# Taking P home earlier: both casts ahead of the exponential, the home transfer ahead of the outgoing one

## The chip, the cores and the metric

One core of one Trainium2 chip. The metric is the device time of one execution in microseconds (us); of the kernel before, three runs gave 974.37, 975.12 and 977.23 us, median 975.12 us. All tables and rows come from one profiled execution of it.

## The reference

Attention with a hashed mask, then a feed-forward block on its result, all in float32:

```python
q, k, v: (4, 8, 768, 64);  proj: (64, 6);  w_in: (512, 2048);  w_out: (2048, 512)
q_bits, k_bits = (q @ proj) > 0, (k @ proj) > 0        # six bits: a bucket of each row
mask   = q_bucket[..., :, None] == k_bucket[..., None, :]
scores = where(mask, q @ k.T / sqrt(64), -1e9)
attn   = exp(scores - max);  attn = attn / (sum(attn) + 1e-9)
x      = (attn @ v).transpose(0, 2, 1, 3).reshape(3072, 512)
h      = x @ w_in
out    = (h * clip(h + 3, 0, 6) / 6) @ w_out
```

## The kernel before

**Tiles and steps.** There are 32 heads (4 batches of 8) with 768 queries each, so 192 tiles of 128 queries, numbered g = 0 to 191; six make a head. The loop at line 1195 runs one step k for each tile, and each step works on several tiles at different stages: the scores of tile k+3 are multiplied on TensorE (PE; `scores`, lines 387 and 389), `lowest(k+2)` copies the scores of tile k+2 out of PSUM on VectorE (DVE) and takes each row's extreme (line 396, into a buffer `p` of which there are two), `exponential(k+2)` makes P of it on ScalarE (ACT, line 408). Products are kept near float32 by splitting each operand into a rounded high part and a low part that holds the rest, and adding the products.

**Turning P.** For the product with V, P has to lie with its keys on the partitions. Up to tile 101 the PE transposes it. From tile GT = 102 on (90 tiles) the DVE and two DMA trips do: `flip(g)` transposes P in blocks of 32 by 32 in place (line 429) and sends it to HBM, 384 KB, into one of four buffers `fd` (the outgoing transfer); `move(g)` brings it back, rearranged, with four transfers of 96 KB each (the home transfer, lines 442 to 448) into one of two SBUF buffers, named `spare` and `px` in the profile. Then `split_p(g, c)` splits each half: ACT casts the high part (line 475), and the low part is subtracted on GpSimd (POOL, line 477) for half c = 1 and on DVE (line 479, kept in `lows` until `split_lows` issues it) for c = 0. Two tiles together go to `values_whole` (line 505), twelve matmuls at line 513 at the beginning of an odd step, that use the high parts of half 1 first, then those of half 0, then the low parts.

**What runs beside.** In the same steps the feed-forward block of earlier rows runs, one of sixteen slices of the hidden width a step: `gemm1` (line 661), the gate (ACT at line 683, DVE at line 684), its split into `gb` (ACT at line 689, DVE at line 690), `gemm2` (lines 699, 700, 704). It is a generator in four stages: A is the split of the gate, B is `gemm1`, C is `gemm2` of the slice before together with the gate, D is side work for the next chunk of rows. After the attention ends, the rest of the feed-forward block runs alone.

**Order.** PE, DVE, ACT and POOL run in the order in which the code calls them (line 1099). All plain DMAs are issued by SyncE (SP, line 78) from one queue, in an order that a planner works out by its own estimates; `tc.issue_after(x)` obliges it to put what the block issues behind x in that queue. SP issues in order: when an instruction waits for its semaphores, all that is queued behind it waits too. Waits follow from the data: the home transfer of tile g waits for the landing of its `fd`, and for the low parts of tile g-2, which sat in the same SBUF buffer; `lowest(g)` waits until the outgoing transfer of tile g-2 has read its `p` buffer.

**One step before the change** (`beside_ffn`, line 1115, k > 102) calls, in this order: `values_whole` in odd steps; `lowest(k+2)` and then stage A (the other way round in steps with k % 6 == 2, `behind`); `exponential(k+2)`; side multiplies; `flip(k+2)` with its outgoing transfer; the cast and POOL's low part of half 1 of tile k-1; stage B; outputs; stage C, inside which (`amid`, between the gate's two instructions) the cast of half 0 and DVE's low part come; `lead(k+3)` with the scores; `move(k+1)`, tied behind the outgoing transfer of tile k+2; stage D.

Of the kernel before, what the change touches and what calls it, by code (L numbers as in the profile page):

```python
# [28 lines left out]
LA = 3  # L29
# [3 lines left out]
LT = 1  # L33
# [10 lines left out]
def lsh_attention_moe(  # L44
# [10 lines left out]
    nc = tc.nc  # L55
# [3 lines left out]
    KT = S // P  # L59
# [14 lines left out]
    last = None  # L74

    def dma(out: bass.AP, in_: bass.AP):
        nonlocal last
        last = nc.sync.dma_start(out=out, in_=in_)  # L78

    paced = False  # L80
# [147 lines left out]
    NS = NJ * KT  # L228
# [3 lines left out]
    GT = GF + FT  # L232
# [139 lines left out]
    scs, probs, outs = {}, {}, {}  # L372
# [18 lines left out]
    def lowest(g: int):  # L391

        s = scs.pop(g)
        m = sp.tile([P, 1], F32, name=f"m{g}", tag="m", bufs=4)
        pr_ = sp.tile([P, 2, HW], F32, name=f"p{g}", tag="p", bufs=2)
        nc.vector.tensor_scalar(  # L396
            out=pr_[:], in0=s[:, :, :HW], scalar1=CAP, scalar2=None,
            op0=ALU.min, op1=ALU.min, accum_out=m[:],
        )
        probs[g] = pr_, m  # L400
# [20 lines left out]

    written, moved, homes = {}, {}, []

    def flip(g: int):
        nonlocal written
        x = probs.pop(g)[0][:].rearrange("p c k -> p (c k)")
        nc.vector.transpose(x, x)  # L429
        d = dp.tile([P, S], F32, name=f"fd{g}", tag="fd", bufs=4)  # L430
        dma(out=d[:], in_=x)
        written[g] = d, last

    def move(g: int):
        if not homes:
            px = sp.tile([P, S], F32, name="px", tag="ga", bufs=1)
            homes.extend([spare[0][:, :S], px[:]])
        to = moved[g] = homes[g % 2]
        d, _ = written.pop(g)
        after = written[g + 1][1] if g + 1 in written else last  # L440
        with tc.issue_after(after.ins):
            for x in range(4):
                r = slice(32 * x, 32 * x + 32)
                dma(
                    out=to[r].rearrange("b (i c) -> b i c", i=4),
                    in_=d[:].rearrange("(i b) (g c) -> g b i c", i=4, g=4)[x],
                )

    lent = []

# [32 lines left out]
    def split_lows():  # L483
        for f in lows:
            f()
        lows.clear()
# [31 lines left out]
    adds, fresh = [], []  # L518
# [10 lines left out]
    def output(un: int):  # L529
        nonlocal vdone  # L530
        i, u = divmod(un, KT // 2)
        b, h = divmod(i, H)
        o = (h % 2) * D
        acc = accs.pop(un)

        if u != 1:
            outs[i] = sp.tile([P, 4 * P if u == 0 else 2 * P], F32, name=f"y{i}_{u}", tag=f"y{u}", bufs=1)
        y = outs[i][:, 2 * P :] if u == 1 else outs[i][:, : 2 * P]

        r = slice(o, o + D)  # L540
        r2 = slice(D - o, 2 * D - o)
        last_head = h == H - 1 and u == (0 if b else 2)
        if last_head:
            nc.scalar.copy(y[r], acc[r2])
            nc.vector.tensor_add(y[r], acc[r], y[r])
        else:
            nc.scalar.copy(y, acc[:])
        if u or last_head:
            single = last_head or h == H - 1 and b
            c = slice(2 * u * P, 2 * (u + 1) * P) if single else slice(0, 4 * P) if u == 1 else slice(4 * P, S)  # L550
            to = xs[b][h * D : (h + 1) * D, c]

            with tc.issue_after(copied.ins):
                dma(out=to, in_=y[r] if single else outs[i][r])
            if not last_head:
                ts = (u,) if single or u else (0, 1)
                (fresh if single and u == 2 else adds).append((i, ts if u != 1 or single else (0, 1), to, y[r2] if single else outs[i][r2]))
        vdone = 2 * un + 2


# [118 lines left out]
    def gate(n: str, fc: int, hg, copy, engine, between=lambda: None):  # L679

        hp, g = hg[:, 0], hg[:, 1]
        r = sp.tile([P, TC], F32, name=f"g{n}_{fc}", tag="g", bufs=1)
        nc.scalar.activation(r[:], hp, AF.Relu, bias=three[:], scale=1.0)  # L683
        nc.vector.scalar_tensor_tensor(out=g, in0=r[:], scalar=6.0, in1=hp, op0=ALU.min, op1=ALU.mult)  # L684
        between()

        def split():
            gh, gl = gate_tiles(f"{n}_{fc}")
            copy(gh, g)  # L689
            engine.tensor_sub(gl, g, gh.bitcast(F32))  # L690
            return gh, gl

        return split
# [31 lines left out]


    xr0, x0 = {}, {}
    side, opening, amid = [], [], []

    def beside():  # L730
        if side:
# [195 lines left out]
    def ffn():  # L927
# [5 lines left out]
        def there(c: int) -> bool:  # L933

            b, t = chunks[c]
            return vdone >= (b + 1) * HK - KT + 2 * (t + 1) and not pending(b, range(H), t)
# [40 lines left out]
        for c, (b, t) in enumerate(chunks):  # L977
            while not there(c):
                if pend is not None:
                    finish()()  # L980
                stage = "B"
                yield
            n = f"{b}_{t}"
            if c not in xr:
                begin(c)
            while side:
                beside()
                stage = "B"
                yield
                if not paced:  # L990
                    yield
            if c not in xhl:
                place(c)
                for cc in range(NCC):
                    split(c, cc)
            ffn_on = True
            copy = nc.scalar.copy
            po = None
            for fc in range(NFC):
                hp = gemm1(n, fc, xhl[c])  # L1000
                stage = "C"
                yield
                end = finish() if pend is not None else lambda: None
                if po is None:
                    po = ps.tile([P, 2, 512], F32, name=f"po{n}", tag="s" if b == B - 1 and t % 2 == 0 else "po", bufs=1)
                parted = paced
                split_g = gate(n, fc, hp, copy, nc.vector, lambda: amid and amid.pop()())
                if not parted:
                    gg = split_g()
                end()  # L1010
                if c + 1 < len(chunks) and c + 1 not in xr and there(c + 1):
                    if fc >= XF[chunks[c + 1][0] == B - 1]:
                        begin(c + 1)
                if parted:
                    stage = "D"
                    yield
                    for _ in range(-(-len(side) // (NFC - fc))):
                        beside()
                if fc + 1 == NFC and c + 1 in xr and c + 1 not in xhl and not side:
                    place(c + 1)  # L1020
                    for cc in range(NCC):
                        split(c + 1, cc)
                elif not parted:
                    beside()
                if parted:
                    stage = "A"
                    yield
                    gg = split_g()
                pend = ((b, t), (fc, [po[:, u] for u in range(2)], *gg))
                stage = "B"  # L1030
                yield
                if not parted:
                    beside()
            del xhl[c]
# [64 lines left out]
    with tc.manual_schedule(engines={ET.PE, ET.DVE, ET.Activation, ET.Pool}):  # L1099
# [15 lines left out]
        def beside_ffn(k: int):  # L1115
# [9 lines left out]
            for _ in range(2):  # L1125
                u = vnext // 2
# [6 lines left out]
                        through.append(vnext // 2 - 1)  # L1133
                if k < GT:
                    break
            behind = (k - 1 + LA) % KT == 4
            if GT <= k < NS - 2 and not behind:
                lowest(k + 2)
            go("A")
            if GT <= k < NS - 2 and behind:  # L1140
                lowest(k + 2)
            if k < GT:
                for c in range(2):
                    split_p(k, c, False)
                split_lows()
                while through:
                    output(through.pop(0))
                flip(k + 1)
# [9 lines left out]
            paced = True  # L1158
            multiply()
            if k + 2 < NS:  # L1160
                flip(k + 2)
            split = GT <= k - LT < NS
            if split:
                split_p(k - LT, 1, False)
            go("B")
            if k == NS + LT:
                homes.clear()
# [2 lines left out]
            hashed = k + LA < NS and (k + LA) % KT == 4 and (k + LA) // KT + 1 < NJ  # L1170
            if hashed:
                hash_qk((k + LA) // KT + 1)
            if split:
                amid.append(lambda: (split_p(k - LT, 0, False), split_lows()))
            go("C")
            while amid:
                amid.pop()()
            split_lows()
            if hashed:
                bits((k + LA) // KT + 1)  # L1180
            if k + LA < NS:
                lead(k + LA)
            if moves:
                moves.pop(0)()
            if GT <= k + 1 < NS:
                move(k + 1)

            place_in_chunk = (k - GT) % NFC
# [6 lines left out]
        for k in range(NS + LT + 2):  # L1195
# [4 lines left out]
            i, t = divmod(k, KT)  # L1200
# [74 lines left out]
        paced = False  # L1275
# [52 lines left out]
```

## Time and profile before

| | |
|---|---|
| three runs | 974.37, 975.12, 977.23 us |
| profiled execution | 973.11 us, span of its instructions 971.3 us |
| PE / weight loads / DVE / ACT / POOL busy | 948.0 / 873.6 / 723.5 / 625.0 / 473.6 us |
| stage with flips, 396.2 to 799.8 us | 90 flips, PE busy 396.77 of 403.60 us, DMA engines busy 0.82 |
| DMA traffic | 152.06 MB, mean 157 GB/s |

The PE row says how long matmuls were under way by a model of their ends, and the granted clock is 0.998 of the full one. The stage from 396.2 us to 799.8 us is the one that the change touches: 90 of the 192 steps. A row of the timeline gives the start and the length in us, then engine, line, operation, the tile written and the tile read, the shapes, how many instructions are merged into the row, and, in square brackets, how long the engine had been idle before and what ended that. DMA rows of SP are the issue of a transfer, not the transfer.

### The profile page before, as it was taken

The page shows a single profiled execution, that of the slowest core. Times are in us where ns is not written, and L with a number is a line of the kernel's source. Part 1 is how long each engine was busy: PE and PEld are TensorE (multiplying, and loading weights), DVE is VectorE, ACT ScalarE, POOL GpSimd, SP SyncE. Part 2 cuts the span into 40 slices and gives each one's busy share as a digit, 9 for nine tenths or more (in the row PEclk, how much of TensorE's full clock was granted, in tenths as well). Part 3 has the DMA queues.
Part 4 walks back from the last instruction along what each step waited for, and adds up shares of the span by engine and source line. Part 5 has one row for each costly group of instructions (what it writes and reads, how often), then busy time and mean ns, then how long its engine had stood idle before and what let it go on. Part 6 is the DMA issues. An engine that isn't in the chain of part 4 may idle for free.

```text
span 971.3 us, 19460 instructions
## 1 busy us (share of the span) xinstructions
PE 948.0 (98%) x6306; PEld 873.6 (90%) x6306; DVE 723.5 (74%) x1470; ACT 625.0 (64%) x1421; POOL 473.6 (49%) x582
## 2 busy tenths in 40 slices
PE   8999999999999999899999999999999999999997
PEld 7999888999989999799899899989899899889896
DVE  7999988888569999877878878878777874342422
ACT  6898875655478988667766666666666664333332
POOL 6777744665537776455555545555545432000000
PEclk9999999999999999999999999999999999999999
DMA  3567579100035554787898788788887772101000
GB/s 117 140 156 188 131 224 377 58 1 1 6 119 119 115 142 112 192 252 233 238 267 234 231 256 241 230 267 236 243 258 233 211 227 71 44 1 44 1 22 22
DMA packets 113613, 152.06 MB, mean 157 GB/s; under 512 B 13876, under 2 KB 82612, under 8 KB 113512
## 3 DMA queue, kind: packets, MB, share of 16 engines
q1 hardware_dynamic: 108472, 144.79, 48.8%
q0 software_dynamic: 5040, 6.03, 5.3%
q8 instruction: 50, 0.82, 0.4%
q14 instruction: 51, 0.42, 0.2%
HBM read 77.34 MB, written 54.00 MB: 135 GB/s over the span
## 4 chain that ended last, share of the span: by engine, by line
PE 79%; DVE 8%; DMA 4%; ACT 4%; issue 3%; POOL 1%; SPq 1%; ACTq 0%; DVEq 0%; POOLq 0%
PE h L661 25%; PE acc L500 6%; PE po L704 6%; PE po L699 6%; PE po L700 6%; PE acc L513 6%; PE pt L418 5%; PE s L389 5%; PE s L387 5%; DMA spare<-fd 2%; DVE p L396 2%; DVE pl L479 2%; ACT ph L475 1%; SPq L78 1%; DVE qq L352 1%
## 5 line engine op out<-in xcount | busy, mean ns | idle before, releaser
L408 ACT ACTIVATE p<-p,m 128x768 f32<-128x768 f32 x192 | 180.2, 939 | 113.4 <-DVE p L396 105.2
L396 DVE TENSOR_SCALAR_CACHE_REDUCE p<-s 128x768 f32<-128x768 f32 x192 | 182.7, 952 | 24.9 <-PE pt L418 12.4
L684 DVE SCALAR_TENSOR_TENSOR h<-g,h 128x256 f32<-128x256 f32 x192 | 81.1, 423 | 102.0 <-ACT g L683 99.0
L683 ACT ACTIVATE g<-h,three 128x256 f32<-128x256 f32 x192 | 91.2, 475 | 94.9 <-PE h L661 94.0
L661 PE MATMUL h<-xh,w 128*128 128x256 f32 x1024 | 146.8, 282 | 0.0
L661 PEld LDWEIGHTS h<-xh,w 128*128 128x128 f32 x1024 | 134.9, 188 | 4.2 <-ACT xh L650 0.6
L429 DVE STREAM_TRANSPOSE p<-p 128x768 f32<-128x768 f32 x90 | 88.1, 979 | 65.2 <-ACT p L408 65.1
L477 POOL TENSOR_TENSOR pl<-spare,ph 128x384 fp32r<-128x384 f32 x45 | 45.8, 1018 | 127.3 <-ACT ph L475 71.4
L479 DVE TENSOR_TENSOR pl<-pt,ph 128x384 fp32r<-128x384 f32 x196 | 100.0, 550 | 4.0 <-ACT ph L475 3.5
L387 PE MATMUL s<-kk,qq 76*128 76x384 f32 x384 | 100.5, 343 | 2.0 <-ACT kk L357 1.5
L389 PE MATMUL s<-kk,qq 128*128 128x384 f32 x384 | 100.4, 343 | 0.0
L700 PE MATMUL po<-w,gb 128*128 128x512 f32 x250 | 98.4, 393 | 0.0
L699 PE MATMUL po<-w,gb 128*128 128x512 f32 x250 | 98.3, 393 | 0.0
L475 ACT CAST ph<-pt 128x384 fp32r<-128x384 f32 x196 | 86.1, 474 | 14.3 <-PE pt L418 13.0
L216 POOL TENSOR_TENSOR w<-wr,w 128x128 fp32r<-128x128 f32 x128 | 71.9, 593 | 45.2 <-ACT w L210 41.9
L418 PE MATMUL pt<-ident,p 128*128 128x128 f32 x612 | 86.2, 275 | 1.9 <-DVE pl L479 1.1
L689 ACT CAST gb<-h 128x256 fp32r<-128x256 f32 x141 | 52.4, 372 | 54.5 <-DVE h L684 26.8
L661 PE MATMUL h<-xl,w 128*128 128x256 f32 x512 | 81.2, 280 | 0.0
L418 PEld LDWEIGHTS pt<-ident,p 128*128 128x128 f32 x612 | 72.5, 141 | 8.9 <-PE pt L418 1.5
L704 PE MATMUL po<-w,gb 128*128 128x512 f32 x250 | 78.6, 395 | 1.5 <-DVE gb L690 1.5
L318 POOL TENSOR_TENSOR kk<-raw,qq 64x192 fp32r<-64x192 f32 (+1 forms) x73 | 65.4, 920 | 25.1 <-ACT qq L304 21.7
L387 PEld LDWEIGHTS s<-kk,qq 76*128 76x128 f32 x384 | 66.6, 190 | 11.7 <-ACT kk L357 2.0
(153 smaller groups left out, 2150.9 us busy)
## 6 DMA issues: line engine op xcount, KB each, us to landing
fd<-p SPq DMA_DIRECT2D x90, 384.0 KB
spare<-fd SPq DMA_DIRECT2D x180, 96.0 KB
px<-fd SPq DMA_DIRECT2D x180, 96.0 KB
kk<-qq SPq DMA_DIRECT2D x62, 192.0 KB
wr<-in_w_in SPq DMA_DIRECT2D x16, 512.0 KB
wr<-in_w_out SPq DMA_DIRECT2D x16, 512.0 KB
raw<-in_qkT SPq DMA_DIRECT2D x19, 384.0 KB
vr<-in_v SPq DMA_DIRECT2D x32, 192.0 KB
```

The lines of the kernel that those rows point to most:

```text
L387: nc.tensor.matmul(s[:, c, :HW], lhsT=q1[:KM, us], rhs=half(k1[:KM], c), start=True, stop=False)
L389: nc.tensor.matmul(s[:, c, :HW], lhsT=q2[:, us], rhs=half(k2, c), start=False, stop=True)
L396: nc.vector.tensor_scalar(out=pr_[:], in0=s[:, :, :HW], scalar1=CAP, scalar2=None, op0=ALU.min, op1=ALU.min, accum_out=m[:],)
L408: nc.scalar.activation(pr_[:], pr_[:], AF.Exp, bias=m[:], scale=-1.0, accum_out=sms[b][:, t, h : h + 1])
L418: nc.tensor.transpose(pt[:, x], probs[g][0][:, c, x * P : (x + 1) * P], ident[:])
L475: nc.scalar.copy(hi, pt)
L479: lows.append(lambda: engine.tensor_sub(lo, pt, hi.bitcast(F32)))
L661: nc.tensor.matmul(hp, lhsT=wi[:, wp, wc], rhs=x[cc][xp], start=(k == 0 and cc == 0), stop=(k == 2 and cc == NCC - 1),)
L683: nc.scalar.activation(r[:], hp, AF.Relu, bias=three[:], scale=1.0)
L699: nc.tensor.matmul(po[u], lhsT=gh[:, us], rhs=wo[:, 0], start=(fc == 0), stop=False)
L700: nc.tensor.matmul(po[u], lhsT=gh[:, us], rhs=wo[:, 1], start=False, stop=False)
L704: nc.tensor.matmul(po[u], lhsT=gl[:, us], rhs=wo[:, 0], start=False, stop=(fc == NFC - 1))
```

## The change

Inside the steps k > 103, `halves_of(k-1)` now stands ahead of `exponential(k+2)`: both casts, POOL's low part of half 1 and DVE's of half 0. Right behind it `move(k+1)` issues the home transfer, so that it stands ahead of `flip(k+2)`, and `brought` ties the outgoing transfer of tile k+2 behind the last of the four home transfers. Before, the home transfer was tied behind that outgoing transfer. In step 103 the casts stay at the end of the step, and stage A comes ahead of `lowest(105)`. `amid` and its place in the gate go. The adding DMA of the last third of a batch's last head isn't held back by a turn any more in the stage beside the feed-forward block.

```diff
-    written, moved, homes = {}, {}, []
+    written, moved, homes, brought = {}, {}, [], []
     def flip(g: int):
...
-        dma(out=d[:], in_=x)
+        if brought:
+            with tc.issue_after(brought.pop().ins):
+                dma(out=d[:], in_=x)
+        else:
+            dma(out=d[:], in_=x)
         written[g] = d, last
     def move(g: int):
...
+        brought[:] = [last]
...
-                (fresh if single and u == 2 else adds).append(
+                (fresh if single and u == 2 and not paced else adds).append(
...
-                split_g = gate(n, fc, hp, copy, nc.vector, lambda: amid and amid.pop()())
+                split_g = gate(n, fc, hp, copy, nc.vector)
...
-            behind = (k - 1 + LA) % KT == 4
+            behind = (k - 1 + LA) % KT == 4 or k == GT + 1
             if GT <= k < NS - 2 and not behind:
                 lowest(k + 2)
             go("A")
             if GT <= k < NS - 2 and behind:
                 lowest(k + 2)
+            def halves_of(g: int):
+                for c in (1, 0):
+                    split_p(g, c, False)
+                split_lows()
+            split = GT <= k - LT < NS
+            if split and k - LT > GT:
+                halves_of(k - LT)
+                if k + 1 < NS:
+                    move(k + 1)
...
             if k + 2 < NS:
                 flip(k + 2)
-            split = GT <= k - LT < NS
-            if split:
-                split_p(k - LT, 1, False)
             go("B")
...
-            if split:
-                amid.append(lambda: (split_p(k - LT, 0, False), split_lows()))
             go("C")
-            while amid:
-                amid.pop()()
-            split_lows()
             if hashed:
                 bits((k + LA) // KT + 1)
+            if split and k - LT == GT:
+                halves_of(GT)
             if k + LA < NS:
                 lead(k + LA)
             if moves:
                 moves.pop(0)()
-            if GT <= k + 1 < NS:
+            if GT <= k + 1 < NS and not (split and k - LT > GT):
                 move(k + 1)
```

More of the change, by code (lines that the diff above doesn't have):

```diff
@@ L556, in output @@
                 ts = (u,) if single or u else (0, 1)
-                (fresh if single and u == 2 else adds).append((i, ts if u != 1 or single else (0, 1), to, y[r2] if single else outs[i][r2]))
+                (fresh if single and u == 2 and not paced else adds).append((i, ts if u != 1 or single else (0, 1), to, y[r2] if single else outs[i][r2]))
         vdone = 2 * un + 2
@@ L727, in lsh_attention_moe @@
     xr0, x0 = {}, {}
-    side, opening, amid = [], [], []
+    side, opening = [], []
     def beside():
```

## The prediction

> **What bounds the kernel now.** I read first the windows of busy time for the stage that the change touches, with the row of the flips, then what PE waited for in that stage.
>
> ```profile
> 396.20:799.80 403.60, 396.77 (x2573) 365.58 (x2572) 319.54 (x611) 268.02 (x628) 208.26 (x269) 1.00 0.82 241
> ```
>
> ```profile
> L429 DVE STREAM_TRANSPOSE p<-p x90: 968/978/982, 396.2 to 799.8; 128x768 f32<-128x768 f32 x90
> ```
>
> ```profile
> PE acc L513 <- ACT ph L475: 4.5, 9, 1.5
> PE po L704 <- DVE gb L690: 1.5, 2, 0.8
> PE z L334 <- ACT y L547: 0.2, 1, 0.2
> ```
>
> The first row is a stretch, its length, then the busy time of PE, weight loads, DVE, ACT and POOL, the clock, and the share of the DMA engines and GB/s. PE is busy for 396.77 of 403.60 us at the full clock, so it sets the pace; a step takes (799.8 - 396.2) / 89 = 4.535 us on average. All that PE waits for in this stage is 4.5 + 1.5 + 0.2 = 6.2 us, most of it the value matmuls waiting for ACT's casts, in nine of the 45 pairs. No rearrangement of ACT, DVE or SP can win more than about these 6 to 7 us. What it can lose is open, since the DMA engines are busy at 0.82 beside PE's 0.98.
>
> The timeline of one whole step (and the edges of its neighbours) shows the order:
>
> ```profile
> 604.09 0.51 ACT L475 CAST ph<-px 128x384 fp32r<-128x384 f32 x1
> ...
> 604.44 0.54 SPq L78 DMA_DIRECT2D fd<-p  x1
> ...
> 604.63 0.56 DVE L479 TENSOR_TENSOR pl<-px,ph 128x384 fp32r<-128x384 f32 x1
> ...
> 604.66 0.96 PE L513 MATMUL acc<-ph,vv 128*128 128x256 f32 x6
> ...
> 605.11 0.95 DVE L396 TENSOR_SCALAR_CACHE_REDUCE p<-s 128x768 f32<-128x768 f32 x1
> 605.24 0.36 ACT L689 CAST gb<-h 128x256 fp32r<-128x256 f32 x1
> 605.25 1.80 SPq L78 DMA_DIRECT2D px<-fd  x4
> ...
> 605.98 0.42 DVE L690 TENSOR_TENSOR gb<-h,gb 128x256 fp32r<-128x256 f32 x1
> ...
> 606.10 0.94 ACT L408 ACTIVATE p<-p,m 128x768 f32<-128x768 f32 x1 [0.50 <-DVE p L396]
> ...
> 607.03 0.50 ACT L475 CAST ph<-spare 128x384 fp32r<-128x384 f32 x1
> ...
> 607.16 0.98 DVE L429 STREAM_TRANSPOSE p<-p 128x768 f32<-128x768 f32 x1 [0.43 <-ACT p L408]
> ...
> 607.61 1.01 POOL L477 TENSOR_TENSOR pl<-spare,ph 128x384 fp32r<-128x384 f32 x1 [2.16 <-DMA px<-fd]
> ...
> 607.83 0.47 ACT L683 ACTIVATE g<-h,three 128x256 f32<-128x256 f32 x1 [0.30 <-PE h L661]
> ...
> 608.17 0.34 SPq L78 DMA_DIRECT2D fd<-p  x1
> 608.20 0.50 ACT L475 CAST ph<-spare 128x384 fp32r<-128x384 f32 x1
> ...
> 608.34 0.43 DVE L684 SCALAR_TENSOR_TENSOR h<-g,h 128x256 f32<-128x256 f32 x1 [0.20 <-ACT g L683]
> ...
> 608.74 0.56 DVE L479 TENSOR_TENSOR pl<-spare,ph 128x384 fp32r<-128x384 f32 x1
> ...
> 609.34 0.37 ACT L689 CAST gb<-h 128x256 fp32r<-128x256 f32 x1
> ...
> 609.87 0.96 DVE L396 TENSOR_SCALAR_CACHE_REDUCE p<-s 128x768 f32<-128x768 f32 x1 [0.57 <-PE s L389]
> ...
> 610.75 0.42 DVE L690 TENSOR_TENSOR gb<-h,gb 128x256 fp32r<-128x256 f32 x1
> ...
> 612.22 0.62 PE L704 MATMUL po<-w,gb 128*128 128x512 f32 x2
> ```
>
> Three things are to be seen. The cast of half 0 ends at 604.60 us and the value matmuls begin at 604.66: there is no slack, hence the nine waits. The home transfer is issued at 605.25 us, 0.06 us after the low part of its buffer ends (604.63 + 0.56 = 605.19). And the outgoing transfer of the step (604.44) stands before it on SP, so the two big transfers of a step overlap and neither waits for the other.
>
> **Part one: the casts and low parts move up.** No instruction is added: 2 x 0.50 us of ACT, 1.01 of POOL and 0.56 of DVE a step stand elsewhere. In the step above, ACT ends the gate's split at 605.60 and was idle for 0.50 us before the exponential; with the two casts there the exponential begins at about 606.6, 0.5 us late. DVE puts its low part behind line 690 and ends it at about 607.2 and the side multiply at 607.6; the flip begins at 607.7 for 607.16, also 0.5 late. The gate's first half waits for PE until 607.83 and ACT is free by 607.75, so it isn't late; its second half goes from 608.34 to 608.66, and the next split of the gate on ACT came at 609.34, so this 0.3 us is covered. If that cover were gone, it would cost 0.3 us in each of some 75 ordinary steps, 22 us. The casts now lie a half step and more ahead of the value matmuls, so the 4.5 us of PE's waits for them go. Part one is worth -4.5 us.
>
> **Part two: stage A ahead of `lowest(105)`, and the adding DMA.** At 405.08 us below, PE waits 0.80 us for a low part of the gate that stood behind a `lowest`; the swap in step 103 takes that wait away: -0.8 us. The adding DMA of one head goes out at the end of step 147 instead of 151, on POOL, which is busy for 208.26 of 403.60 us: nothing. The tail after 800 us is untouched.
>
> **Part three: the home transfer ahead of the outgoing one.** Four issues of SP are moved past one, and with them a wait. Before, SP issued "outgoing of tile k+2, home of tile k+1". After, it is "home of k+1, outgoing of k+2", and the home transfer of k+1 reads the `fd` that was sent out one step earlier, so SP stops until it has landed. That closes a ring with one step a turn: outgoing issue, its landing (L), four home issues, next outgoing issue. A step can't be shorter than L + reaction + four issues. Before, a whole home transfer and another outgoing one lay between, so the ring wasn't closed.
>
> The four issues, and a last store for a lower bound, from the rows of line 78:
>
> ```profile
> L78 SPq DMA_DIRECT2D spare<-fd x180: 302/442/887, 400.8 to 803.1; - x180
> L78 SPq DMA_DIRECT2D px<-fd x180: 302/448/2137, 404.0 to 805.9; - x180
> ...
> L78 SPq DMA_DIRECT2D out<-ob x18: 341/378/807, 269.1 to 968.2; - x18
> ```
>
> The median is 0.442 to 0.448 us, so four take 1.78 us (the row at 605.25: 1.80). The reaction is 0.06 us (604.63 + 0.56 to 605.25).
>
> L isn't a row of its own. It is read where something waited for it:
>
> ```profile
> 400.37 0.32 SPq L78 DMA_DIRECT2D fd<-p  x1
> 400.78 1.93 SPq L78 DMA_DIRECT2D spare<-fd  x4
> ...
> 403.72 0.96 DVE L396 TENSOR_SCALAR_CACHE_REDUCE p<-s 128x768 f32<-128x768 f32 x1 [0.45 <-DMA fd<-p]
> ...
> 405.08 0.73 PE L704 MATMUL po<-w,gb 128*128 128x512 f32 x2 [0.80 <-DVE gb L690]
> ```
>
> ```profile
> 456.37 0.53 SPq L78 DMA_DIRECT2D fd<-p  x1
> 457.00 3.26 SPq L78 DMA_DIRECT2D px<-fd  x4
> 460.36 0.38 SPq L78 DMA_DIRECT2D fd<-p  x1
> 461.68 1.25 SPq L78 DMA_DIRECT2D spare<-fd  x3
> ```
>
> ```profile
> SPq L78 <- DMA fd<-p: 0.8, 1, 0.8
> ```
>
> ```profile
> GB/s 0 0 0 0 0 0 0 0 0 0 0 0 0 0 0 0 216 402 448 371 402 140 77 309 448 433 371 325 16 0 0 0 0 0 0 0 0 0 0 0
> ```
>
> At 403.72 the DVE is released by a landing 403.72 - 400.37 = 3.35 us after its issue, with a home transfer pressing on right behind it. The third fence is what SP waited for between 460 and 463 us: the home transfer at 461.68 had waited 0.8 us for the `fd` issued at 456.37, so that L was 5.3 us, with four slow home issues and a second outgoing transfer in between. The last row is the traffic from 966 us to the end at 971.3 in 40 slices: the last store of 256 KB, issued at 968.2, has its last bytes in slice 29, at 966 + 29 x 0.1325 = 969.8, so even alone a smaller transfer took 1.6 us and its receipt.
>
> So L lies between 1.6 and 5.3 us, and the ring between 1.6 + 0.06 + 4 x 0.302 = 2.9 us (it never binds) and 5.3 + 0.06 + 1.78 = 7.1 us (+223 us). I take L = 3.0, near the 3.35: in the new order no home transfer presses on behind, but the four just issued run ahead of it. The ring is then 3.0 + 0.06 + 1.78 = 4.84 us, above the 4.535 of a step. Of the 87 home transfers in the new order (tiles 105 to 191) each step is longer by 0.305 us: 26.5 us. The first steps are absorbed: an outgoing transfer at 604.44 has until 609.87, when `lowest` takes its buffer, which is 5.43 - 3.0 = 2.4 us to spare, and the gate's low part (ends 611.17) is needed at 612.22, another 1.0; about 3 us in all. Behind that the casts wait for the home transfer, the exponential and the gate's first half stand behind the casts on ACT, and `gemm2` on PE waits for the gate; PE's 4.5 + 0.8 us of old waits then lie inside the longer step and can't be counted again. SP's other transfers (loads of q, k, v, x, the row copies) stand behind the waiting one too, and where the planner puts one between the four, its issue joins the ring.
>
> The Trainium skill, "DMA: Bandwidth & Descriptors", section "Rules for kernel authors", advises to issue a DMA early and wait on its semaphore late; the change does the opposite to the outgoing transfer. The same page of the Trainium skill, section "Anatomy of one DMA — SWDGE (gpsimd) path", has a fit of 2.0 us plus the bytes at 436 GB/s for DMAs that GpSimd issues; as an estimate, 384 KB would take 2.9 us, the ring 4.74 us and the sum 973.11 + 87 x 0.2 - 3 = 987.5 us. The row's 3.35 us lies above that fit.
>
> **Sum.** 973.11 + 26.5 - 3 = 996.6 us against the profiled execution's 973.11 us; the median of the runs is 2.0 us above that execution, so 999 us.
>
> **Rivals.**
>
> The ring doesn't bind (faster). With the DMA engines less crowded at the moment of the outgoing transfer, L would be 2.6 us or less and the ring 4.44 us, under the 4.535. From L = 2.7 (4.535 - 1.84) on downward only parts one and two are left: 973.11 - 4.5 - 0.8 = 967.8, with the runs' 2.0 about 970 us, and down to 966 with the other waits. For it: the last store's 1.6 us, and the steps with hashing, which are longer and let the ring catch up. Against: the 3.35 us in the row that is nearest, and the 3.26 us that four home issues took at 457.00.
>
> The two cancel (no change). At L = 2.8 the ring is 4.64 us: 87 x 0.105 = 9, less 3 absorbed, is 6 us later if the old waits are inside, and about even if part of them is still won: 973 to 979.
>
> The moved casts cost by themselves (slower, without the ring). If ACT's exponential being 0.5 us late reaches the gate after all, the 0.3 us of part one come due in 75 steps, less the 5.3 won: 973.11 + 22 - 5 + 2 = 992 us. Against it: 0.5 us between the gate's end and the next split on ACT.
>
> **How the numbers follow.** The ring that binds: 0.60. The ring that doesn't: 0.24. The cancelling: 0.08. The casts by themselves: 0.08. A change of under 0.3%, 2.9 us, can't be told from none here. That gives faster 0.24, same 0.08, slower 0.68. For the ring that binds, L = 2.85 gives 4.69 us and +10 (985 us), L = 3.4 gives 5.24 us and +58 (1033 us): 985 to 1033. The range for all, 967 to 1033, takes in the side on which the ring doesn't bind, and leaves out L above 3.4.
>
> **What would show it.** Right: SP's wait for `fd` grows from a few us to some 100 us or more; the spacing of the flips goes from 4.535 to about 4.8 us; ACT's casts wait for DMA of `spare` or `px`; PE waits at lines 699 or 704 for the gate; the DMA share falls. The wait of line 513 for the casts is gone in any case; if it is still there, part one is wrong. If the flips keep 4.5 us and SP has time left behind its wait for `fd`, the ring doesn't bind and L was taken too long. If the flips are slower while SP waits for low parts or flips instead of `fd`, the casts are to blame.

## The result and the profile after

The changed kernel takes 1027.64 us (six runs, 1022.45 to 1029.62) against 975.26 us of the kernel before (six runs, 974.37 to 977.23): a ratio of 1.0525, 95% interval 1.0496 to 1.0554. Its profiled execution took 1022.45 us with a span of 1020.7 us. It is 49.3 us longer than the profiled execution before, and the stage with the flips holds nearly all of that. First the windows of busy time for that stage of the changed kernel (stretch, length, then PE, weight loads, DVE, ACT, POOL, clock, DMA share, GB/s), and its flips:

```profile
397.00:848.00 451.00, 411.92 (x2576) 366.68 (x2575) 321.23 (x612) 273.75 (x629) 208.02 (x271) 0.98 0.73 215
```

```profile
L429 DVE STREAM_TRANSPOSE p<-p x90: 964/978/981, 397.1 to 848.2; 128x768 f32<-128x768 f32 x90
```

The flips are (848.2 - 397.1) / 89 = 5.069 us apart for 4.535 before, and 89 x 0.534 = 47.5 us is the difference of the stage. ACT, DVE and POOL are busy for about as long as before, PE for 15 us longer; the DMA engines' share fell from 0.82 to 0.73. The granted clock is 0.98 in this stage for 1.00 before, but that can't be the main cost: in the run with the gate first, below, it is 1.00 in the stage, and the loss is 47 us for 52. Now what SP, DVE, ACT and PE waited for in the stage of the changed kernel (us in total, times, longest). Lines behind 430 have moved by five at most: 475, 479, 690 and 704 are now 480, 484, 695 and 709.

```profile
SPq L78 <- DMA fd<-p: 112.1, 71, 4.4
```

```profile
DVE p L396 <- DMA fd<-p: 95.2, 59, 3.6
```

```profile
ACT ph L480 <- DMA px<-fd: 13.0, 14, 2.1
ACT ph L480 <- DMA spare<-fd: 12.4, 13, 1.9
```

```profile
PE po L709 <- DVE gb L695: 25.3, 27, 3.1
PE z L334 <- DVE gb L695: 6.1, 8, 2.5
...
PE acc L518 <- POOL pl L482: 0.7, 1, 0.7
```

The first two of these rows in the kernel before:

```profile
SPq L78 <- DMA fd<-p: 3.2, 6, 0.8
```

```profile
DVE p L396 <- DMA fd<-p: 0.5, 1, 0.5
```

SP's wait for outgoing transfers went from 3.2 us in six waits to 112.1 us in 71. The value matmuls (now line 518) no longer wait for ACT's casts. PE waits instead for the gate's low part (line 695), which stands on DVE behind a `lowest` that waits for the outgoing transfer. One turn of the ring in the timeline of the changed kernel:

```profile
516.75 0.38 SPq L78 DMA_DIRECT2D fd<-p  x1
516.99 0.98 DVE L429 STREAM_TRANSPOSE p<-p 128x768 f32<-128x768 f32 x1 [0.29 <-ACT p L408]
...
517.69 0.60 SPq L78 DMA_DIRECT2D kk<-qq  x1
...
519.64 1.73 SPq L78 DMA_DIRECT2D px<-fd  x4
519.65 0.96 DVE L396 TENSOR_SCALAR_CACHE_REDUCE p<-s 128x768 f32<-128x768 f32 x1 [1.36 <-DMA fd<-p]
...
521.47 0.38 SPq L78 DMA_DIRECT2D fd<-p  x1
```

The outgoing transfer issued at 516.75 lands at 519.51, by its semaphore events. SP has had nothing else to issue since 518.29 and waits for this landing: the home transfer that reads the buffer goes out at 519.64, 0.13 us behind it, and `lowest` begins on DVE at 519.65, behind the same landing. The flip of 516.99 ended at 517.97, but its own outgoing transfer stands behind the home transfer and goes out at 521.47, 3.5 us later. From one outgoing issue to the next it is 4.72 us here and 5.17 us on average, and at no point of this turn did SP wait for a flip.

### The profile page after: what moved, and what is told of

The parts are those of the page before. It is cut to its first block, busy times and chain, and to the rows that moved or that the text cites. A ratio compares the mean times of both kernels' runs of the same rounds, so it can differ in the third digit from the quotient of the medians.

```text
span 1020.7 us, 19507 instructions
## 1 busy us (share of the span) xinstructions
PE 963.4 (94%) x6306; PEld 873.9 (86%) x6306; DVE 726.9 (71%) x1470; ACT 630.2 (62%) x1421; POOL 471.4 (46%) x582
## 4 chain that ended last, share of the span: by engine, by line
PE 54%; DMA 18%; DVE 13%; issue 6%; SPq 5%; POOL 2%; ACT 2%; DVEq 0%; ACTq 0%; POOLq 0%
PE h L666 16%; DMA fd<-p 16%; PE acc L505 6%; PE pt L418 5%; SPq L78 5%; PE po L709 4%; DVE pl L484 4%; PE po L704 4%; PE po L705 4%; PE s L389 3%; PE s L387 3%; DVE p L396 3%; PE acc L518 2%; DMA px<-fd 1%; DVE gb L695 1%
## 5 line engine op out<-in xcount | busy, mean ns | idle before, releaser
L396 DVE TENSOR_SCALAR_CACHE_REDUCE p<-s 128x768 f32<-128x768 f32 x192 | 183.2, 954 | 116.9 <-DMA fd<-p 95.2
L709 PE MATMUL po<-w,gb 128*128 128x512 f32 x250 | 82.4, 411 | 25.3 <-DVE gb L695 25.3
L704 PE MATMUL po<-w,gb 128*128 128x512 f32 x250 | 99.0, 396 | 1.4 <-ACT gb L694 1.3
L705 PE MATMUL po<-w,gb 128*128 128x512 f32 x250 | 98.4, 394 | 0.0
L709 PEld LDWEIGHTS po<-w,gb 128*128 128x128 f32 x250 | 44.4, 188 | 47.6 <-DVE gb L695 39.4
```

The lines of the kernel that those rows point to most:

```text
L396: nc.vector.tensor_scalar(out=pr_[:], in0=s[:, :, :HW], scalar1=CAP, scalar2=None, op0=ALU.min, op1=ALU.min, accum_out=m[:],)
L704: nc.tensor.matmul(po[u], lhsT=gh[:, us], rhs=wo[:, 0], start=(fc == 0), stop=False)
L705: nc.tensor.matmul(po[u], lhsT=gh[:, us], rhs=wo[:, 1], start=False, stop=False)
L709: nc.tensor.matmul(po[u], lhsT=gl[:, us], rhs=wo[:, 0], start=False, stop=(fc == NFC - 1))
```

## The experiments

The ring theory was set against two rivals: that the moved casts cost by themselves, and that only DVE's order behind the two buffers of P costs. Times are medians, beside runs of the kernel before on the same chip.

**The ring opened, the casts kept early.** The home transfer stands behind the flip and its outgoing transfer again:

```diff
                 halves_of(k - LT)
-                if k + 1 < NS:
-                    move(k + 1)
...
                 flip(k + 2)
+            if split and k - LT > GT and k + 1 < NS:
+                move(k + 1)
```

(and `brought` is gone. In the kernel before, `move` was called at the end of the step.)

> Both casts stay ahead of the exponential as in the changed kernel, but the outgoing transfer of the step goes first again and the home transfer is tied behind it, right behind the flip. The theory is a ring on SP: an outgoing transfer, its landing, four home issues, the next outgoing transfer, closed once a step (5.07 us between flips in the changed kernel, 4.54 before). With the ring open it expects 967 to 972 us and flips 4.46 to 4.50 us apart, with the PE's waits at line 513 gone. The rival, that the moved casts delay ACT and DVE by themselves, expects the time to stay near the changed kernel's, 1010 to 1030 us.

Measured: 976.01 us against 974.6 us, ratio 1.0012, interval 1.0000 to 1.0024. The loss of 52 us is gone, so it belongs to the order on SP. But the gain that was expected of the casts isn't there either: the flips are 4.59 us apart and not 4.46 to 4.50. The waits of PE and ACT in this run, and DVE's low part:

```profile
PE po L704 <- DVE gb L690: 2.7, 3, 1.3
PE po L699 <- ACT gb L689: 1.9, 5, 0.6
PE acc L513 <- POOL pl L477: 1.1, 2, 0.7
```

```profile
ACT ph L475 <- DMA px<-fd: 43.5, 35, 2.2
...
ACT ph L475 <- DMA spare<-fd: 9.5, 13, 1.3
```

```profile
L479 DVE TENSOR_TENSOR pl<-spare,ph x45: 1059/1066/1210, 408.5 to 810.9; 128x384 fp32r<-128x384 f32 x45
L479 DVE TENSOR_TENSOR pl<-px,ph x45: 546/1067/1408, 410.9 to 813.7; 128x384 fp32r<-128x384 f32 x45
```

PE's 4.5 us of waiting for casts at line 513 are gone, but its waiting for the gate has grown from 1.5 us to 2.7 + 1.9 us. Standing ahead of the exponential, the casts wait 43.5 + 9.5 us for home transfers, and ACT's exponential and gate wait behind them. And DVE's low part takes 1.07 us (median) where it took 0.56 to 0.64 in the kernel before:

```profile
L479 DVE TENSOR_TENSOR pl<-spare,ph x45: 557/642/869, 407.0 to 808.1; 128x384 fp32r<-128x384 f32 x45
L479 DVE TENSOR_TENSOR pl<-px,ph x45: 557/559/1467, 412.7 to 810.9; 128x384 fp32r<-128x384 f32 x45
```

**Only the order on SP.** The kernel before with the outgoing transfer put behind the home transfer (`last` is the last of its four) from tile 106 on; the casts stay where they were:

```diff
+        if g > GT + 3:
+            waiting.append((g, d, x))
+            return
         dma(out=d[:], in_=x)
...
+    def send():
+        g, d, x = waiting.pop()
+        with tc.issue_after(last.ins):
+            dma(out=d[:], in_=x)
...
                 move(k + 1)
+            if waiting:
+                send()
```

> The kernel before with its casts where they were, and only the order on SP changed: from tile 106 on each outgoing transfer is tied behind the home transfer of the tile ahead of it, at the end of the step. The ring theory expects the changed kernel's pace without its casts, flips 5.0 to 5.3 us apart, 1015 to 1040 us. The rival of the casts expects 975 us.

Measured: 1042.68 us, ratio 1.0694 (1.0676 to 1.0712); its flips:

```profile
L429 DVE STREAM_TRANSPOSE p<-p x90: 968/978/982, 397.7 to 869.1; 128x768 f32<-128x768 f32 x90
```

```profile
SPq L78 <- DMA fd<-p: 93.9, 63, 4.1
```

That is (869.1 - 397.7) / 89 = 5.30 us a step. The order on SP alone makes the whole loss, without any cast moved. It is 15 us more than in the changed kernel. By the semaphore events the landing is 0.10 us longer there, the time from the landing to the first home issue 0.12 and the four issues 0.07; what makes them longer is open (SP's waits for DVE's low parts come to 2.8 us in all).

**Half of the home transfer behind the outgoing one.** `move` is called for two of its four transfers ahead of the exponential and for the other two behind `flip`:

```diff
-                    move(k + 1)
+                    move(k + 1, range(2))
...
                 flip(k + 2)
+            if split and k - LT > GT and k + 1 < NS:
+                move(k + 1, range(2, 4))
```

(and `brought` is emptied behind the second call.)

> The changed kernel with the home transfer cut in two on SP: two of its four transfers ahead of the outgoing one, two behind it. The ring has two issues of 0.44 us less: 5.17 less 0.9 is 4.3 us, under the 4.54 of a step, so the ring theory expects 968 to 982 us. The rival of the casts expects 1010 to 1030 us. A third theory, that only the two buffers of P matter, which come free when the outgoing transfer has left, expects a part of the loss back, 990 to 1010 us.

Measured: 993.35 us, ratio 1.0189 (1.0174 to 1.0204), with 4.81 us between flips. Two thirds of the loss come back, but not all: the time lies outside of the ring theory's range and inside of the third theory's. From one outgoing issue to the next it is 4.87 us instead of the expected 4.3. By the semaphore events the landing, which had been taken as unchanged, is 3.35 us on average here and 3.08 in the changed kernel, with two home transfers now right behind the outgoing one; the first home issue follows 0.41 us behind the landing for 0.16, the two issues take 0.89 and the next outgoing issue comes 0.22 later. In 56 of 86 turns SP is released by the landing. The casts, too, wait longer than in the changed kernel (13.0 + 12.4 us there):

```profile
ACT ph L480 <- DMA px<-fd: 40.5, 31, 2.3
ACT ph L480 <- DMA spare<-fd: 30.8, 29, 3.2
```

How much of the 19 us that are left is the ring and how much is the casts' waiting isn't separated, and this run doesn't tell the third theory from the ring.

**A small transfer in the ring.** 512 bytes to HBM behind the four home transfers:

```diff
+        if g > GT + 2:
+            small(last)
         brought[:] = [last]
...
+        with tc.issue_after(after.ins):
+            dma(out=dm[:], in_=ident[:1])
```

> The changed kernel with one more transfer in the ring: 512 bytes to HBM, read by nobody, behind the four home transfers and ahead of the outgoing one, in 86 steps. The ring theory expects its issue time, 0.35 to 0.55 us a step, in the flips' spacing: 1057 to 1075 us. The rival of the casts expects the changed kernel's 1028 us.

Measured: 1050.54 us, ratio 1.0783 (1.0760 to 1.0806), 23 us over the changed kernel and less than expected.

```profile
L429 DVE STREAM_TRANSPOSE p<-p x90: 964/978/982, 397.2 to 878.2; 128x768 f32<-128x768 f32 x90
```

The flips are 5.40 us apart, 0.34 more. By the semaphore events the gap between the last home issue and the outgoing one grew by 0.33 us, about an issue; the landing became 0.16 us shorter, and the time from it to the first home issue 0.17 longer. Here the profiled execution of the changed kernel, its fastest run, is 30 us under that of this one, while the medians are 23 us apart. A transfer that does nothing costs its issue once a step: that is what a ring does.

**Half of P sent out.** The outgoing transfer takes the first half of P only, and the four home transfers read that half twice; the second half of P is left out of the result.

```diff
-                dma(out=d[:], in_=x)
+                dma(out=d[:, : S // 2], in_=x[:, : S // 2])
...
-                    in_=d[:].rearrange("(i b) (g c) -> g b i c", i=4, g=4)[x],
+                    in_=d[:].rearrange("(i b) (g c) -> g b i c", i=4, g=4)[x % 2],
```

> The changed kernel with only the first half of each turned P sent out, 192 KB for 384, and the same four home transfers, which read that half twice; the second half of P is left out of the result. Only the landing of the outgoing transfer in the ring gets shorter, by the time of 192 KB at the 400 GB/s of the last store, some 0.4 to 0.5 us. The ring theory expects 985 to 1000 us, flips 4.6 to 4.75 us apart. A theory in which the number of transfers and waits on SP counts, and not the landing, expects 1020 to 1030 us.

Measured: 990.83 us, ratio 1.0160 (1.0139 to 1.0181), flips 4.72 us apart. The landing is 2.63 us instead of 3.08 by the semaphore events, and the step 0.35 us shorter with as many transfers on SP. So the landing of the outgoing transfer is a term of the step.

**The gate first on DVE in every step.** `behind = True`, so stage A stands ahead of `lowest` in every step:

> The changed kernel with the split of the gate ahead of lowest on DVE in every step, so that the gate's low part, for which PE waits 25.3 us at line 709, does not stand behind a lowest that waits for the outgoing transfer. The ring theory expects the same spacing of the flips, 5.0 to 5.1 us, and 1018 to 1032 us, with PE waiting elsewhere. The rival, that the loss comes from DVE's order behind the two buffers of P, expects 985 to 1005 us.

Measured: 1022.56 us, ratio 1.0486 (1.0460 to 1.0513).

```profile
PE s L387 <- DVE p L396: 16.1, 19, 1.8
...
PE po L709 <- DVE gb L695: 1.3, 1, 1.3
```

PE's wait of 25.3 us for the gate's low part is down to 1.3 us, and the time hardly moved: PE waits at the scores for the same `lowest`. The place where PE feels the ring can be moved; the ring stays. No run separates SP's wait from `lowest`'s wait by itself, since the same landing ends both, and none has a third buffer of P, which would do that. Two things speak for SP's order. The outgoing transfer in the changed kernel leaves 3.6 us after its flip on average (0.35 before), and a ring through P's buffers has nothing that would hold it there. And such a ring would close every second step, as there are two buffers, so the 0.33 us that the small transfer added ahead of each outgoing one would have cost about half of that a step; they cost 0.34.

**Casts later, for the lost gain.** With the ring open, both casts directly behind the exponential, and DVE's low part behind the flip:

```diff
                 exponential(k + 2)
+            if split and k - LT > GT:
+                halves_of(k - LT)
...
                 flip(k + 2)
+            split_lows()
+            if split and k - LT > GT and k + 1 < NS:
+                move(k + 1)
```

> The open ring (outgoing transfer first, home transfer tied behind it), with both casts directly behind the exponential instead of ahead of it, and DVE's low part behind the flip. With the casts ahead of the exponential ACT waited 43.5 us for px and 9.5 us for spare, which took back what PE had won at line 513. If that is the reason, casts 0.95 us later wait for less than 15 us in all, and PE's 4.5 us are won: 968 to 973 us. If the waits at line 513 were not worth their 4.5 us, it stays at 974 to 977 us.

Measured: 985.42 us, ratio 1.0102 (1.0085 to 1.0119): neither of the two. The waits for home transfers are gone from the casts, and the time is 10 us longer. DVE's low part takes 0.99 to 1.03 us here too. In this trace the six matmuls on the high parts take 6.3 us less over 44 pairs than before (from start to start), but the steps from the high to the low parts take 7.2 us more and those among the low parts 3.1 more: PE no longer waits for the high parts and meets the low parts' lateness instead.

**Both low parts on DVE.** The open ring with the casts early, and POOL's subtraction given to DVE:

```diff
-            if c:
-                engine = nc.gpsimd
```

> The open ring with the casts ahead of the exponential (974 to 978 us), and the low part of half 1 taken on DVE too, so that POOL subtracts nothing while DVE does. In the open ring DVE's low part took 1.07 us beside POOL's, 0.55 to 0.56 us alone in the kernel before. If the two engines slow each other, both subtractions on DVE take 0.55 us each, 1.1 in all, and the time stays at 972 to 979 us. If the 1.07 us comes from something else, such as the transfers under way, they take 1.0 us each and the time goes to 990 us and over.

Measured: 976.91 us, ratio 1.0010 (0.9995 to 1.0024). The subtraction in this run:

```profile
L477 DVE TENSOR_TENSOR pl<-spare,ph x90: 540/552/1377, 409.6 to 811.7; 128x384 fp32r<-128x384 f32 x90
L477 DVE TENSOR_TENSOR pl<-px,ph x90: 541/554/1376, 411.8 to 814.2; 128x384 fp32r<-128x384 f32 x90
```

(Line 477 is the former 479.) Each takes 0.55 us, so both take 1.1 us, as long as the one did beside POOL's. It was POOL's subtraction that made DVE's slow, not the transfers.

**One cast moved.** The kernel before with the cast of half 0 directly behind that of half 1:

```diff
                 split_p(k - LT, 1, False)
+                split_p(k - LT, 0, False)
...
-                amid.append(lambda: (split_p(k - LT, 0, False), split_lows()))
+                amid.append(split_lows)
```

> The kernel before with one cast moved: that of half 0 stands directly behind that of half 1, behind the exponential and the flip and ahead of the gate's first instruction; both low parts and the order on SP stay. In the run with both casts behind the exponential, DVE's low part had come up beside POOL's and took 1.0 us, and the time was 985 us. If that overlap was the cost, this one keeps 0.56 to 0.65 us for it and wins the waits at line 513: 969 to 974 us. If the earlier cast costs by holding up the gate on ACT, 980 to 986 us again.

Measured: 989.79 us, ratio 1.0141 (1.0117 to 1.0164).

```profile
PE acc L513 <- DVE pl L479: 6.0, 17, 1.3
...
PE acc L513 <- ACT ph L475: 1.8, 5, 0.6
```

```profile
DVE h L684 <- ACT g L683: 58.3, 105, 2.6
```

In the kernel before the last of these rows was:

```profile
DVE h L684 <- ACT g L683: 10.2, 13, 2.6
```

DVE's low part is at 0.55 us here, so the overlap with POOL isn't what costs. The cast stands ahead of the gate on ACT: DVE's second half of the gate waits 58.3 us in 105 steps for the first (10.2 us in 13 before), and the low part comes behind it. The matmuls among the low parts take 15.2 us more over 44 pairs, those among the high parts 7.0 less. No version that was run beats the kernel before.

## Why the prediction was right or wrong

**What bounds the kernel.** That no more than 6 to 7 us can be won wasn't contradicted, as no run won any; that they could be won by earlier casts was wrong.

**Part three, the ring.** The mechanism, the sign and the path were right: SP waits for `fd`, the casts wait for `spare` and `px`, the flips spread, the DMA share falls. The forecast was +24 us and the result is +52 us; the step that failed is the sum "3.0 + 0.06 + 1.78 = 4.84 us". By the semaphore events of 86 turns in the changed kernel's trace (issue and completion of each outgoing and home transfer) it is 3.08 for the landing, 0.16 from the landing to the first home issue, 1.83 for the four issues and 0.09 from there to the next outgoing issue, 5.17 us before rounding. These four fill the time from one outgoing issue to the next whatever its cause. That the ring sets it shows in the second: in 78 of the 86 turns SP issues the first home transfer within 0.2 us of the landing, in the kernel before in 6. The landing was nearly right, and for the reason given, as far as the runs show: in the kernel before, with a home transfer right behind, the landings of the same tiles took 3.44 us on average. Mis-sized were the reaction (0.10 short; the 0.06 was taken from a wait for a DVE instruction, and behind a landing the median is 0.13), the gap between the last home issue and the next one (left out, 0.09), the landing (0.08) and the four issues (0.05). Each is small, but the step's excess over 4.535 is itself only 0.3 to 0.6 us, so that 0.33 us doubled it. The same turns take 4.580 us in the kernel before and 5.166 here: 86 x 0.586 = 50 us, for 49.3 between the two profiled executions. With a sum so near a threshold, what is left out of the ring counts fully. That the result lies within the forecast's 985 to 1033 us is luck: the upper end stood for a landing of 3.4 us, and the landing stayed at 3.08.

**Who passes the ring on.** The text had `lowest`'s buffer among the slack and expected the casts to stop first. In the trace `lowest` waits 95.2 us and the casts 25.4 us. PE's waits for the gate are as forecast, for its low part and not for `gemm2`'s first matmuls.

**Part one, the casts.** PE's waits at line 513 did go, as forecast, but "-4.5 us" was wrong: the open ring, which has parts one and two and an earlier call of `move`, is 1.4 us slower than the kernel before at the median, 0.0 to 0.24%. Two steps failed. The casts' new place was held against the time of the exponential, not against the landing of their own home transfer, for which they then wait 53 us. And "1.01 of POOL and 0.56 of DVE stand elsewhere" took their lengths over, while the two now run side by side:

```profile
603.57 1.09 POOL L477 TENSOR_TENSOR pl<-px,ph 128x384 fp32r<-128x384 f32 x1
...
603.93 1.16 DVE L479 TENSOR_TENSOR pl<-px,ph 128x384 fp32r<-128x384 f32 x1 [0.34 <-ACT ph L475]
```

In this pair of the open ring DVE's subtraction ends 0.43 us after POOL's, after 1.16 us of its own, and alone it takes 0.55: most of its work comes after POOL's end. The Trainium skill, "SBUF — State Buffer", section "SBUF: two separate sides", says that a DVE instruction with two SBUF inputs and a GpSimd instruction that reads SBUF exclude each other for the whole instruction, whoever starts first. The runs agree where POOL starts first, as it does here (1.07 us beside POOL, 0.55 without it), apart from some 0.1 us by which DVE ends sooner than such a lock would let it; spans on POOL are rough. It speaks against this change, and the prediction didn't weigh it.

**Part two.** The swap in step 103 was to win 0.8 us. In the open ring, which has it, the wait that ended at 405.08 us is gone, but PE waits 0.30 us for `lowest` (until 404.75) and 0.53 us for the gate (until 407.65) instead, and the next wait for the gate's low part is 1.32 us (until 410.16) for 0.74 before. Nothing was won that these times could show. The adding DMA was not run by itself.

**The rivals.** That the ring doesn't bind is refuted by the ring-closed run without moved casts (1042.68 us) and by the small transfer. That the casts cost by themselves is refuted for the changed kernel by the open ring, though the two runs with the casts at a later place, each with a cast in front of the gate, were 10 and 14 us slower than the kernel before.

## What to carry to other kernels

On a queue that issues in order, look for rings: if transfer B waits for A's landing and the next A is queued behind B, the step is at least the landing plus every issue between, however idle the engines are. Before a transfer is moved ahead of another, add up that ring with all of its gaps, and be wary when it comes near the step's length. And when work is moved up to remove a wait, check what it depends on and what will run beside it at the new place; a wait for one operand may only be hiding the next one.

## What the runs showed of the hardware

**Beside an instruction load, a landing took 1 us longer.** In the changed kernel a 16 KB instruction load began between 0.5 us before and 2.5 us after the issue of 14 of 85 outgoing transfers. They landed in 3.93 us on average, the 71 others in 2.92. In the kernel before it was 4.17 us (13 of 85) and 3.31, in the run with only the order on SP changed 4.40 us (12 of 85) and 2.98. A landing shows as 16 steps of its semaphore. The fifteenth came after 2.86 us with a load and 2.79 without, so it is one part in sixteen that is late. DMA traffic from 509.75 to 514.7 us in 40 slices, an outgoing transfer from issue to landing:

```profile
GB/s 261 193 155 217 285 224 100 124 312 304 379 379 403 428 372 372 372 224 50 50 25 248 205 236 205 205 161 205 99 25 25 25 25 25 25 25 25 25 25 25
...
q8 instruction: 1, 0.02, 2.3%
```

Slices 22 to 29 hold another transfer, issued at 511.23. In the last eleven, 1.4 us, only 25 GB/s are left, about a sixteenth of the 400 of the middle; the fifteenth step of this landing came after 2.79 us and the last after 4.88. In a ring such a delay comes due each time; as an estimate, 14 x 1.0 = 14 us of the loss go with these loads. That the load is the cause is read from the coincidence and was not tested: some landings beside a load were as short as the others (2.60 us).

**Two subtractions on two engines took as long as both on one.** DVE's low part beside POOL's took 1.07 us, and both on DVE 0.55 + 0.55 us, at the same time for the kernel (976.0 and 976.9 us).
